# Two-stage attention with gated experts: four scored experts per token in more batches, and a new order of the program

## The chip, the core and the metric

The kernel runs on one core of one Trainium2 chip. The metric is device time in microseconds (us), as a median of runs. The engines of the core are named as in the profile: PE (matrix products, with PEld for its weight loads), DVE, ACT and POOL (elementwise work), and SP, whose queue issues all the DMAs.

## What is computed

```python
# x (8, 8, 512, 64), state (8, 8, 32, 64): attention both ways per batch and head
a = softmax(scale * x @ state.T);   xread = a @ state        # 512 rows
a2 = softmax(scale * state @ x.T);  sread = a2 @ x           # 32 rows
x = concat([xread, sread], axis=2) -> (8, 544, 512)          # B, S, D
# then per batch: four experts, of which each token takes the best two of its gate
logits = x @ w_gate; topk = 2 best; w = softmax over the 2 chosen
for e in range(4):
    q, k, v = x @ wq[e], x @ wk[e], x @ wv[e]                # 64 wide
    ye = softmax(causal(scale * q @ k.T)) @ v @ wo[e]
    out += (e chosen by the token) * w_of_that_choice * ye
```

The weights wq and wk are 200 times larger than drawn, so products are made from two float16 halves (high and low) in three matmuls: high*high, high*low, low*high.

## The kernel before

There are eight batches. A batch has 512 tokens in four query tiles of 128, numbered i = 0 to 3, and 32 rows of the state read, which are gathered over two batches into a tail. A batch goes through a **front** (state attention, products with the combined weights, the gate, the keys `kt`, the queries `qm`, the values `v`), a **main** part (scores, softmax, transposition, reads, output product) and a **side** (the state's own reads). The parts of neighbouring batches are interleaved.

In the main part, `probs` (L916) makes the score products of a *unit* into two PSUM banks. A *lane* of a unit is one query tile i against its 128*(i+1) keys. On each lane DVE adds the causal mask and takes the maximum (`masked`, L397, which writes `p`), ACT takes the exponential (`p<-p,mx`), and `split` (L338) writes high and low halves into `ph`: the high half on ACT, POOL or DVE, the low half on POOL or DVE. One DMA transposes `ph` into `pt`. `reads` (L957) multiplies `pt` with `v`, DVE or ACT scales the sums into `z`, and `result` (L1015) multiplies with `wo_n` and stores `o`.

There are two ways to score a tile, and `units_of` (L493) says which batch takes which:

```python
def units_of(b):
    if b < CFG["D1"]:
        units = [((0, "s"), (1, "s")), ((2, "s"),), ((3, "s"),)]
    elif b < CFG["DA"]:
        units = [((1, "d"),), ((0, "s"), (2, "s")), ((3, "s"),)]
    else:
        units = [((1, "d"),), ((0, "0"), (2, "0")), ((0, "1"), (2, "1")), ((3, "0"),), ((3, "1"),)]
    return units
```

- **Slots** ("s"): a token's two chosen experts sit in two slots, so a tile has two lanes. The query of a slot is a row of three candidates of which two are zeroed by the gate: DVE or ACT multiplies the product with the mask `m` (`qf`), `split` makes halves (`qh`), and a DMA transposes them into `qm`. A tile has 6 score matmuls of 128 rows and 6 of 64 rows, each 128*(i+1) columns wide (two of 64 rows run side by side on PE). A read per key tile is 6 matmuls of 194 columns.
- **All four** ("d", "0", "1"): a tile has four lanes, one for each expert ("0" and "1" are two of them each), and the weights of the two that were not chosen are zero only at the end. A tile's 12 score matmuls are all of 64 rows, the queries of a whole batch come straight from the product in transposed form, without `m`, `qf` and DMA, and a read per key tile is 12 matmuls of 65 columns.

`D1=6, DA=6` in `CFG` gives slots to batches 0 to 5 and all four to batches 6 and 7. A run of `st.run` (L255) issues the steps in a fixed order: the three strings in `ORDER` (L22) hold the order of the steps, which of several engines does a step that can go to more than one, and which buffer each tile takes. `FILL` (L511) lists matmuls on zeros that may be put where PE has nothing to do at the start.

Of the kernel before, what the change touches and what calls it, by code (L numbers as in the profile page):

```python
# [18 lines left out]
CFG = dict(FILL=(1.0, 1.4, 1.8, 2.2, 2.6, 3.0, 3.4, 3.8, 4.2, 4.6, 5.0,), RA=-1, RG=1, RV=2, RK=2, ZL=3, GP=1, PT=4, ZM=4, SM=4, QM=4, SIDE=32, FB=1, PX=1, PA=2, LB=1, xn=4, W0=-33, PACE=37.0, MU=2, XP=(1,), QP=(0,), LAG=2,
           FRONT=1.5, FSPAN=1.0, TSPAN=1.3, TOFF=1.2, KT=3, p32=3, ph=2, at=1, et=1, gs=1, xh=4, a2=1, o=4, sn=1, qf=2,  # L20
           n_eb=1, n_e2=1, n_a2t=1, n_xt_tail=2, n_z32=3, n_z=2, n_zh=2, n_tq=1, n_tv=2, n_tpt=1, n_tz=1, n_pt=3, D1=6, DA=6)
ORDER = (  # L22
    (
        "c-jrsgJKYB7y!`E|CZKJE!P@qORFurZM9|Fwr$(CZQHhO+xETZB~AhGf-H~^d>}CdKyHW+QIHkFAR%OiypRYALk0+ef{+!90RRF4gMdORh=A"
        "0P4c9;#NC2xK1`K>*E%-wcaF7E0AT1<^valLb!U`w@)u9CB#AQ$eGQkPRjiC^M<scbEVo4|uh4B<5g_>{@Vxa;Q!J?Q8D?%-(1o`na1VUvv1"
        "KFVpTmWx44+o$&cz`FwgQ}1ROTk%a0CnIT)P-u07cW9XD2Dam5~PDhPzYK>F31A~ur$<%Ah-+#aXG}n73cta;VNu_?AR6Z;WcOronR{z!f<Q"
        "`9ibZpLw86IyFh3^^ne`L4q8BGXah<sVFC7p=CBTWL1Wkr8=)`shJLUQx<C|ef<CYio4_{c4~wukUWWm&0T$zSxB*RJ1nhulya`KjGYo`sI0"
        ")9m5^N8zXfU*d@;C|dLn{~pBVi}RU^X}kbD#nifuXPrnTA0L91as;3QPo|Junvz!g8DpqhJNzf~hbXR^l|62dmJFO5$|zq%klb?!s-ThzlSd"
        "y`-^_17^TNh)<Pp7R-ckkbq`GeH;&oX%WQYF}M$L=uN9}F)V>K_y&Ba6gI$z;7d#45j=*qcn=;xWvqdB;0e5ir|=d0s0u!Vcklw<LrqLb&*3"
        "<HgjM_!>R>}`jHU4de1}?C6<<Lk{03#P2_~X-SR2b?HEfEX;0IL4pU@gV!$<0X>+w6iqh{C^JK+ZGh(D+ecE#rSo_;}RY=K7Yur9uaZs@2b_"  # L30
        "QLkq7kgtr^q~IO2kYSg9Eja<5N^c5cnG@S5Zr`AaTrd(;rIn6ViKB(sc5qFz~3+hKhRX1gst!o%)+EJ8z-Z~WYiO<VM-c<f5D&T;B-t)9+-k"
        "gU>cf>GcY;*15ZqfpC}#zj>NPy598x!8jFbO=nIWQ!UUL&I?;ISOpNm}J$0c`_?1FwGztb#SK5p}DGOzwWSE_@QW%BPVR%gexCOW2H_Ac&sJ"
        "I>9&{o`mdoUpelHpEFgu5|022nTKg-753?!{nwOF1b8W~LRq52MHn4`K#9guf_+QsPPMPJieyW~BYtgN|S(B0h@0sSfp|V;G3YLHL)BBXAL7"
        "Ud@TI82zJQ6h48)sVwKAx^x;#Pz06Z@_Y)XNH3~KA*ft|qbVcCQhiE=MX4g6LE}uAk9yNqPK~$l9D3sp&PCh!EEb^k97&E#QVfOSPR>i`@g;"
        "8H{8W${P;T1Jn|KX3q&T{Sx3Lth<#KcfUtxbL4zKYpUdGb&2G{Wwyo#II7k6<bPJ`F5GMA?^RE5h@1$v8NcpWR!1*}AVIDqb9Wok_~(1SN}W"
        "*kV(XbV@NLR6LdQckEwwWtZb!|L=NYfvL<OO2^8dGbYUPE9E>_oFscliE=Ws>-z~BgEsC`~iL0n|*K)wIn|tOw~9o4j~_o&qHY#CE!*xoOW}"
        "2>O&(a2`A(k(t-ByNJ`3wI1zuubhwvi%0fBF`}hDK=C9b1YVdx(kJb4I*JOVlO%E`Iyy9;-ib~pS8bf0#8Q;WlG)o@hc=F<-oKimFJep6hIh"
        "D+zB)CXE;|h9&spUH!;|VlR=2CuMEGucY{J;e?krvSs+DMBjjU?y!a-0`Z0bWH*X%fBVpSYTe!W$0YW%Q0WQwq+&n`kXn)ihj?Q*wIzg~7aq"
        "e&ZZjAX_O9|G^MW%WEhLzvmMi%2|0ig>g1sN11u5War6rl2dVBUQgkik27)(F2?Ej6sMKB@(gowCJy9C2!|;Y!P6v&BY7L;;#jVtx%oL3;?z"
# [1177 lines left out]
```

## Time and profile before

| | |
|---|---|
| median of 3 runs | 281.54 us (281.47 to 282.27) |
| profiled execution, its own time | 282.26 us |
| its span from first to last instruction | 280.5 us |
| time around the span | 1.76 us |
| granted TensorE clock | 1.00 in all of the span |
| PE, DVE, ACT, POOL busy | 96%, 90%, 82%, 60% of the span |

Busy time is the time in which at least one instruction of the engine runs. Durations of single instructions overlap with the next one's on DVE and ACT, so a sum of durations is larger than the busy time. The end of a matmul is modelled, so a start-to-start distance between groups of matmuls says more than a duration.

### The profile page before, as it was taken

What the parts mean: (1) busy time and instruction counts of PE and PEld (TensorE: products, weight loads), DVE (VectorE), ACT (ScalarE), POOL (GpSimd) and SP (SyncE); (2) the same over time, 40 slices, a digit from 0 to 9 for tenths busy, and PEclk for the clock granted to TensorE, in tenths of its full rate; (3) what the DMA queues carried; (4) which work ended last, traced back from release to release, by engine and by line L of the source; (5) the groups of instructions that cost most, each with busy time, mean ns of one, the idle gap of its engine ahead of it and who ended that gap; (6) DMA issues with size and microseconds to landing.
All of it is one profiled execution on the core that took longest, in us unless ns stands there. A gap on an engine that the chain in (4) does not pass through costs nothing.

```text
span 280.5 us, 9087 instructions
## 1 busy us (share of the span) xinstructions
PE 268.0 (96%) x3408; PEld 179.8 (64%) x3408; DVE 251.3 (90%) x749; ACT 229.0 (82%) x629; POOL 169.6 (60%) x234
## 2 busy tenths in 40 slices
PE   6979899899999899999999999999999999999995
PEld 3856666666486564767677566677576855576763
DVE  3599999999999999999999999899889999889852
ACT  3799898999899789899968988987886779877533
POOL 6534667177886787758757976595473587414210
PEclk9999999999999999999999999999999999999999
DMA  6957899999998969999999999995797979999995
GB/s 184 252 110 178 183 173 206 213 199 166 153 245 170 200 153 222 208 225 227 217 148 192 224 212 193 149 209 139 151 152 159 219 138 173 211 185 191 181 260 208
DMA packets 161804, 53.16 MB, mean 190 GB/s; under 512 B 140640, under 2 KB 157280, under 8 KB 161760
## 3 DMA queue, kind: packets, MB, share of 16 engines
q1 hardware_dynamic: 161760, 52.59, 96.7%
q8 instruction: 26, 0.43, 0.7%
q14 instruction: 18, 0.15, 0.2%
HBM read 11.02 MB, written 8.91 MB: 71 GB/s over the span
## 4 chain that ended last, share of the span: by engine, by line
PE 69%; DVE 17%; ACT 6%; DMA 4%; issue 2%; SPq 1%; DVEq 0%
PE bank L265 69%; DMA pt<-ph 2%; DVE gs L265 2%; DVE p L265 2%; DMA xn<-in_x_dram 2%; ACT e L265 1%; DVE xh L265 1%; DVE m L265 1%; DVE sbm L265 1%; DVE z L265 1%; DVE qf L265 1%; ACT qh L265 1%; SPq L265 1%; DVE xt_tail L265 1%; DVE eb L265 1%
## 5 line engine op out<-in xcount | busy, mean ns | idle before, releaser
L265 ACT ACTIVATE p<-p,mx 128x128 f32<-128x128 f32 (+3 forms) x80 | 41.7, 556 | 6.1 <-DVE su L265 2.4
L265 PE MATMUL bank<-gs,at 128*128 128x260 f16 (+3 forms) x320 | 44.0, 284 | 1.3 <-issue 0.8
L265 PE MATMUL bank<-v,pt 128*128 128x194 f16 (+1 forms) x600 | 42.2, 226 | 0.3 <-DMA pt<-ph 0.3
L265 PE MATMUL bank<-kt,qm 64*128 64x128 f16 (+7 forms) x384 | 42.2, 299 | 0.1
L265 PEld LDWEIGHTS <-pt 128*128 128x128 f16 x600 | 38.5, 98 | 4.0 <-issue 0.9
L265 POOL TENSOR_TENSOR ph<-p,ph 128x768 f16<-128x768 f32 (+1 forms) x18 | 34.7, 1925 | 4.7 <-ACT ph L265 2.3
L265 DVE CUSTOM_DVE_ANT_0 p<-bank,band 128x384 f32<-128x384 f32 (+3 forms) x80 | 36.2, 482 | 1.3 <-PE bank L265 1.0
L265 PEld LDWEIGHTS <-at 128*128 128x128 f16 x288 | 27.3, 97 | 7.9 <-issue 2.1
L265 PEld LDWEIGHTS <-qm 64*128 64x128 f16 (+1 forms) x384 | 21.0, 96 | 17.3 <-issue 8.7
L265 PE MATMUL bank<-at,gs 128*128 128x512 f16 (+1 forms) x116 | 30.0, 396 | 0.1
L265 PE MATMUL bank<-wo_n,z 128*128 128x512 f16 (+1 forms) x114 | 26.1, 368 | 0.0
L265 PE MATMUL bank<-wo_n,zp 128*128 128x512 f16 x84 | 20.4, 379 | 0.4 <-DVE xt_tail L265 0.4
L265 POOL TENSOR_TENSOR qh<-qf,qh 128x768 f16<-128x768 f32 x11 | 18.0, 1644 | 4.3 <-ACT qh L265 2.4
L265 ACT ACTIVATE o<-bank 128x512 f32<-128x512 f32 (+1 forms) x27 | 15.4, 578 | 6.4 <-DMA out_dram<-o 3.3
L265 DVE SCALAR_TENSOR_TENSOR xh<-xn,xh 128x512 f16<-128x512 f32 x26 | 18.6, 718 | 0.5 <-ACT xh L265 0.4
L265 ACT ACTIVATE ph<-p 128x1024 f16<-128x1024 f32 (+1 forms) x17 | 16.5, 970 | 1.9 <-DMA pt<-ph 1.8
L265 PEld LDWEIGHTS <-gs 128*128 128x128 f16 x108 | 9.9, 98 | 12.4 <-issue 2.4
L265 PEld LDWEIGHTS <-z 128*128 128x128 f16 x114 | 10.7, 98 | 10.9 <-issue 0.6
L265 ACT ACTIVATE z<-bank,c 128x64 f32<-128x64 f32 x72 | 16.0, 320 | 0.9 <-POOL c L265 0.8
L265 PEld LDWEIGHTS <-xh 128*128 128x128 f16 x416 | 14.0, 98 | 3.4 <-POOL xh L265 1.5
L265 ACT ACTIVATE xh<-xn 128x512 f16<-128x512 f32 x25 | 15.0, 621 | 1.1 <-DMA xn<-in_x_dram 0.7
L265 ACT ACTIVATE gs<-bank 128x260 f16<-128x260 f32 (+2 forms) x32 | 15.2, 500 | 0.5 <-PE bank L265 0.4
(241 smaller groups left out, 655.5 us busy)
## 6 DMA issues: line engine op xcount, KB each, us to landing
out_dram<-o SPq DMA_DIRECT2D x33, 256.0 KB, 3.0
xn<-in_x_dram SPq DMA_DIRECT2D x14, 512.0 KB, 4.6
xn<-in_x_dram SPq DMA_DIRECT2D x4, 256.0 KB, 3.8
sn<-in_state_dram SPq DMA_DIRECT2D x8, 64.0 KB, 3.9
p<-in_moe_wo_dram SPq DMA_DIRECT2D x2, 256.0 KB, 4.6
pt<-ph SPq DMA_TRANSPOSE x28, 4.8
p<-in_moe_wv_dram SPq DMA_DIRECT2D x1, 384.0 KB, 6.0
p<-in_moe_wk_dram SPq DMA_DIRECT2D x1, 384.0 KB, 4.7
```

The lines of the kernel that those rows point to most:

```text
L265: f(**{k: v.ap() if isinstance(v, View) else v for k, v in kw.items()})
```

## The change

`D1` goes from 6 to 3 and `DA` from 6 to 4: batches 0 to 2 keep slots, batch 3 scores tile 1 for all four experts and tiles 0, 2 and 3 by slots, and batches 4 to 7 score all four everywhere. `FILL` gets five more entries (5.4 to 7.0). `ORDER` is another set of strings: all steps may stand elsewhere, on another engine or in another buffer.

```diff
-CFG = dict(FILL=(1.0, 1.4, 1.8, 2.2, 2.6, 3.0, 3.4, 3.8, 4.2, 4.6, 5.0,), RA=-1, ...
+CFG = dict(FILL=(1.0, 1.4, 1.8, 2.2, 2.6, 3.0, 3.4, 3.8, 4.2, 4.6, 5.0, 5.4, 5.8, 6.2, 6.6, 7.0,), RA=-1, ...
-           n_eb=1, ..., n_pt=3, D1=6, DA=6)
+           n_eb=1, ..., n_pt=3, D1=3, DA=4)
 ORDER = (
     (
-        "c-jrsgJKYB7y!`E|CZKJE!P@qORFurZM9|Fwr$(CZQHhO+xETZB~AhGf-H~^d>}CdKyHW+QIHkFAR%OiypRYALk0+ef{+!90RRF4gMdORh=A"
+        "c-jrqgF+Z;7y!`E|JvG`+t%FBTwAM|wQ6pwS=DUYwr$(CZQHiZd(S(Z?2r?ZLTT`avJeKz004o2K|moLL_iAghQyE@0x<)uhLW%b)<SwHfLW"
...
```

What the two orders hold differently, counted over all rows: PE has 132 fewer reads of 194 columns (360 to 228) and 264 more of 65 columns (240 to 504), 48 fewer query products of 256 columns and 24 more of 512, and 5 more filling matmuls of 512 columns (11 to 16). The score matmuls are 384 before and after, but 54 of those with 128 rows become matmuls with 64 rows. The SP queue has 32 transpositions of `ph` for 28 and 6 of `qh` for 10; in blocks of 128 by 128 all transpositions are 1034 for 996.

DVE, the masks of batch 4's first unit before: tiles 0 and 1 by slots (four lanes of 128 and 256 keys, bank pairs by slot; numbers after a name are the buffer's).

```order
L265 ISA p_2_114,mx_163<-bank_83,band 128x128
L265 ISA mx_163 128x1
L265 RECIPROCAL su_172<-su_172 128x2
L265 ISA p_2_114,mx_163<-bank_83,band 128x256
L265 ISA mx_163 128x1
L265 ISA p_2_114,mx_163<-bank_77,band 128x256
L265 ISA mx_163 128x1
L265 ISA p_2_114,mx_163<-bank_77,band 128x128
```

DVE, the masks of batch 4's first unit in the changed program: tile 1 alone with all four experts.

```order
L266 ISA p_1_113,mx_163<-bank_81,band 128x256
L266 ISA mx_163 128x1
L266 ISA p_1_113,mx_163<-bank_81,band 128x256
L266 ISA mx_163 128x1
L266 ISA p_1_113,mx_163<-bank_83,band 128x256
L266 ISA mx_163 128x1
L266 ISA p_1_113,mx_163<-bank_83,band 128x256
L266 ISA mx_163 128x1
L266 TENSOR_TENSOR cmp_126<-lg_122 128x80
```

Four lanes of mixed width have become four of 256 keys, and the batch now has five such units and not three.

ACT, the exponentials of the same unit before, with the high half of `ph` as the last row.

```order
L265 ACTIVATE sbm_119<-sbm_119 128x32
L265 ACTIVATE p_2_114<-p_2_114,mx_163 128x256
L265 ACTIVATE z_1_167<-bank_80,c_0_173 128x64 x6
L265 ACTIVATE kt_137<-bank_81 128x512
L265 ACTIVATE lg_122<-bank_78 128x4
L265 ACTIVATE mx_162<-mx_162 128x2
L265 ACTIVATE lg_122<-bank_82 128x4
L265 ACTIVATE o_178<-bank_77 128x512
L265 ACTIVATE p_1_113<-p_1_113,mx_162 128x384
L265 ACTIVATE p_2_114<-p_2_114,mx_163 128x256
L265 ACTIVATE lg_122<-bank_80 128x4
L265 ACTIVATE ph_156<-p_2_114 128x768
```

ACT, the same unit in the changed program.

```order
L266 ACTIVATE p_1_113<-p_1_113,mx_163 128x256 x2
L266 ACTIVATE xh_94<-xn_89 128x512
L266 ACTIVATE p_1_113<-p_1_113,mx_163 128x256
L266 ACTIVATE xt_tail_154<-bank_84 64x4x32
L266 ACTIVATE o_177<-bank_83 128x512
L266 ACTIVATE p_1_113<-p_1_113,mx_163 128x256
L266 ACTIVATE gt_0_129<-gt_0_129 128x20
L266 ACTIVATE p_2_114<-p_2_114,mx_162 128x384
L266 ACTIVATE xh_94<-xn_89 128x512
L266 ACTIVATE xt_tail_154<-bank_84 64x4x32
L266 ACTIVATE p_2_114<-p_2_114,mx_162 128x384
L266 ACTIVATE ph_156<-p_1_113 128x1024
```

The unit's high half is now 1024 wide and not 768, and the next unit's first exponentials stand ahead of it.

PE at the start of the program before, around the transposition of the state `sn` (`band` is the filling matmul).

```order
L265 MATMUL bank_84<-ident,xn_89 128x128 x4
L265 LDWEIGHTS band
L265 MATMUL bank_83<-band 128x512
L265 MATMUL bank_81<-ident,sn_0_86 128x128 x2
L265 MATMUL bank_80<-ident,xn_90 128x128 x4
```

PE at the same place in the changed program.

```order
L266 MATMUL bank_81<-ident,xn_90 128x128 x4
L266 LDWEIGHTS band
L266 MATMUL bank_82<-band 128x512
L266 LDWEIGHTS band
L266 MATMUL bank_82<-band 128x512
L266 LDWEIGHTS band
L266 MATMUL bank_82<-band 128x512
L266 LDWEIGHTS band
L266 MATMUL bank_82<-band 128x512
L266 LDWEIGHTS band
L266 MATMUL bank_82<-band 128x512
L266 MATMUL bank_84<-ident,sn_0_86 128x128 x2
```

Five filling matmuls stand ahead of the state's transposition where one stood. Further on, ahead of the transposition of `eb`, four stand where three stood.

## Rows read from the trace of the kernel before

**Rows 1.** The page: span, and busy time by engine (share of the span, instructions).
```profile
span 280.5 us, 9087 instructions
PE 268.0 (96%) x3408; PEld 179.8 (64%) x3408; DVE 251.3 (90%) x749; ACT 229.0 (82%) x629; POOL 169.6 (60%) x234
```

**Rows 2.** The chain in order of time: start us, length us, engine and tile.
```profile
154.81 55.43 PE bank L265 x581
...
215.87 24.45 PE bank L265 x341
```

**Rows 3.** Stretches: length; busy PE, PEld, DVE, ACT, POOL; clock, DMA share, GB/s.
```profile
40.00:104.00 64.00, 60.64 (x810) 41.20 (x811) 62.50 (x174) 58.91 (x169) 44.22 (x50) 1.00 1.05 188
104.00:253.00 149.00, 148.18 (x1859) 98.54 (x1858) 139.70 (x441) 124.15 (x347) 98.31 (x118) 1.00 0.99 188
253.00:280.00 27.00, 24.35 (x278) 16.00 (x276) 18.23 (x61) 13.65 (x37) 5.38 (x10) 1.00 0.96 215
...
50.00:90.00 40.00, 38.30 (x472) 26.10 (x471) 38.90 (x111) 37.91 (x115) 26.79 (x32) 1.00 1.09 191
40.00:140.00 100.00, 96.59 (x1222) 64.51 (x1222) 97.85 (x279) 91.23 (x256) 71.46 (x81) 1.00 1.07 199
```

**Rows 4.** PE in order of time: start us, length us, op, out<-in, columns, count.
```profile
200.29 2.21 PE L265 MATMUL bank<-kt,qm 128*128 128x512 f16 x12
202.34 0.28 PE L265 MATMUL bank<-tl,rep 64*128 64x4 f32 x2
...
207.28 2.17 PE L265 MATMUL bank<-v,pt 128*128 128x194 f16 x24
209.39 0.83 PE L265 MATMUL bank<-kt,qm 64*128 64x256 f16 x12
...
237.88 1.63 PE L265 MATMUL bank<-v,pt 128*128 128x65 f16 x48
239.45 1.47 PE L265 MATMUL bank<-kt,qm 64*128 64x512 f16 x12
240.85 1.47 PE L265 MATMUL bank<-wo_n,z 128*128 128x512 f16 x6
```

**Rows 5.** Groups by form: out<-in, shapes, count | busy us, mean ns | idle before.
```profile
L265 ACT ACTIVATE ph<-p 128x1024 f16<-128x1024 f32 x10 | 10.6, 1062 | 1.8 <-DMA pt<-ph 1.8
L265 ACT ACTIVATE p<-p,mx 128x512 f32<-128x512 f32 x20 | 14.0, 721 | 0.2
L265 ACT ACTIVATE p<-p,mx 128x128 f32<-128x128 f32 x20 | 7.6, 395 | 2.0 <-DVE mx L265 1.1 <-POOL mx L265 0.8
L265 ACT ACTIVATE o<-bank 128x512 f32<-128x512 f32 x25 | 14.6, 594 | 6.0 <-DMA out_dram<-o 3.3 <-PE bank L265 2.7
L265 ACT ACTIVATE qf<-bank,m 128x64 f32<-128x64 f32 x36 | 8.0, 320 | 1.0 <-PE bank L265 0.7 <-DVE m L265 0.3
L265 DVE CUSTOM_DVE_ANT_0 p<-bank,band 128x512 f32<-128x512 f32 x20 | 13.2, 681 | 0.2 <-PE bank L265 0.2
L265 DVE CUSTOM_DVE_ANT_0 p<-bank,band 128x128 f32<-128x128 f32 x20 | 5.6, 283 | 0.4 <-PE bank L265 0.4
L265 DVE TENSOR_SCALAR o<-bank 128x512 f32<-128x512 f32 x8 | 5.5, 683 | 0.3 <-PE bank L265 0.3
L265 POOL TENSOR_TENSOR ph<-p,ph 128x1024 f16<-128x1024 f32 x9 | 19.2, 2132 | 0.9 <-ACT ph L265 0.8
L265 POOL TENSOR_TENSOR qh<-qf,qh 128x768 f16<-128x768 f32 x11 | 18.0, 1644 | 4.3 <-ACT qh L265 2.4 <-DVE qh L265 1.7
L265 PEld LDWEIGHTS <-pt 128*128 128x128 f16 x600 | 38.5, 98 | 4.0 <-issue 0.9 <-DMA pt<-ph 0.4
```

**Rows 6.** PE at the start, in order of time, with its idle time before.
```profile
5.44 0.38 PE L265 MATMUL bank<-band 128*128 128x512 bf16 x1 [0.23 <-ACT xT L265]
6.56 0.44 PE L265 MATMUL bank<-ident,sn 128*128 128x128 f32 x2 [0.74 <-ACT sn L265]
...
17.03 0.66 PE L265 MATMUL bank<-ident,eb 128*128 128x128 f32 x4 [1.16 <-DVE eb L265]
```

**Rows 7.** The only matmul that waited for a transposition, and these transpositions' landing (us).
```profile
248.23 0.91 PE L265 MATMUL bank<-v,pt 128*128 128x65 f16 x24 [0.32 <-DMA pt<-ph]
...
pt<-ph SPq DMA_TRANSPOSE x28, 4.8
```

More of the change, by code (lines that the diff above doesn't have):

```diff
@@ L17 @@
 AX = mybir.AxisListType
[L19 removed]
+CFG = dict(FILL=(1.0, 1.4, 1.8, 2.2, 2.6, 3.0, 3.4, 3.8, 4.2, 4.6, 5.0, 5.4, 5.8, 6.2, 6.6, 7.0,), RA=-1, RG=1, RV=2, RK=2, ZL=3, GP=1, PT=4, ZM=4, SM=4, QM=4, SIDE=32, FB=1, PX=1, PA=2, LB=1, xn=4, W0=-33, PACE=37.0, MU=2, XP=(1,), QP=(0,), LAG=2,
@@ L25 @@
[L25 to L39, printed above, removed]
@@ new lines @@
+        "mgRDdLq5eyu}0}qG~sbC#sg4D1P(m-0s3<;nb_<;{pgdE@tQIG|yLkLDgD4vD-Py;GKF{}#3u_lzmLKp%KpcI~mhHwsQK^WGC3(yGaz(u$Mk"
+        "x&9l;#G(NPe=%fzzga^X-o;1;3zbO!gv`fLp>-4*PsZ-LNmAyaj+lCU~{+u9pEOchboW@8bfQi1)CupibGj!0%hPf9D-i36}G_^XbVNL4HU#"
+        "<upPR>4#*Ghs5cydPS6e7!9fVZ7SJAou_Nq(Q!ohngQHfk2{yn|><l|$07T$&90+$H99zO&=mLFUFf7B}a1X}95QtAhAqrREK3Ik2u`gtUaW"
+        "D)#XctU`l^Bf`a5bKW;m{A>(+D^W-C;V6go?NZk3az!1#59M%!H{h25R6msD$gV2i%8QP#Gt|45*1!a5jvGTDTY1<78M2Jz*g{f(cLx=0I{<"
+        "0#l$W#-q8g2<F2)NJPh>0WJV9S_)5~HpXINS_Vm|4mQNc5Q#6~0mR`mXoN|r2|k4lxRsy7LuiamF&S;dYPcL)U|n1RFJUFThI&{XTVgZ(2zg"
@@ new lines @@
+        "->dQ)?J1NHG06ouT-3VY!hcnc}$9ejqA)D=@vYmCA7unImw2TV<Uunm5JZrB}r<2U#P9dQtTg>sO924jEx07Gy94#e*;6o=stXp5c{3O#T*Z"
+        "pIP#2Rh*v{tY9sGtR?N_?brI7@UfKVJ3FLX*eIhP*40u3vd?xq@R$GrsF~c{7z|T5eCBy%mV??7yrQrT8v*QBaOwh)DJ(>Y|KPIs2z^Od@u)"
+        "ns68TPriu86eo;C~Pvg-OeQ611ARqiq3Gpvwq3)Cjz3>ywMZ&~50rOE0+JaeW8}_6?nuLN|F&p)w{4^Q=kv}ED>{Nh)$&aRBA?i&9Nil$u;t"
+        "4QJi$RnQ9j3<|6c3Z(c07tFfiWi?M-SYA8Soh9`akPA%!qq%C!WAf+=q7KD#=aRF%zD`z7!ubBl1b?M|tQp5<AXI%$-&E0w%y+XuKDTlkyq#"
+        "!+6|;qWJ*sM_=quHFzK9z=Ghx2QfM3#6wt<<MUap#knwocJg`5jU{M5$5LU~#kIL2?cu|ifOm6Kx`>6TGF73X6iS{vh)Pm3I>1#aj`ngMtVE"
@@ new lines @@
+        "6J2<FAoRF>Z1AudnFs2mNZB2<Q=D3a=MG_90slnP5xb*e${u_lGkL9Rs~ur7C?)c6rQQEjS2b*UcJrv`KhxAA3cPFb)84WNNkfev$P%7<65G"
+        "u_AST#vKjRoua!uqB028!8VSDFr6vecXx?u|FQ+F7yCXVng!cBJdeg@I&lM*YFEAq5!PVk1&Q(aX1a9#GH~-^L1=XNw^z%^9WieN4Xs(<r}y"
+        "~hR|aiNy+#o9_I#p3)jnS97Ut)7@y%Wbb?RwSZYsa`6S=LU-%V&<0<}wTcwMpk>tEV((q7vf<8Qq#!*_{E<VzbpW;S&hUs`SPoT82fX?xFN`"
+        "sB~8&0J3Jc(j>GOeX4w1^hdR9Z+&=sc&BZBl}l(lpv3D`+`g;AOOuw$UoekLhKTl;n&27ccQ@x{IaxAFii$v{Op)2Fk#fc@yoR)l!Cmkh1f1"
+        "+D>caJFb-s;>-7Nvt;C*<i{H+7iW}Rw1%$m56r@4IX7>n8I+&%aRJUG{v5~wT#$n}nDcNUevU+$xI7o;yquMHQ&BF*#dsza=Mc`p**KIda|P"
@@ new lines @@
+        "Z)IXR4HQAKWMRk$kelFU4tA~~F|GSe-N;A(u0_tS0uiF>3v&!Ih3iC^PxIY61^E+3@5bcgp!Hry}QIf`H40lC2k<qaO99xCK3_jn)elbd`<v"
+        "Wn7iDg=k=ung3f7|SOJwV#rnr2EX;gd1}^j^hX1lzVGOJtC*5ziy>wEP9%b&{65B$)%}1;$zZ+AG2zE?#<2lxOC!Hd_r1sM;@RLxixp-N0dV"
+        "Pa4$VWow*x#;WpftUvM_@mb3JVvq)P$N~TZvG4<pAJV=vBAAQC_@Py9M04~C>`6(TvRPu}xi8nfZ$w{TJKBtuOhLg!a9>nJ*o_fhUPAy;fq$"
+        "HN}^nowPC3!)o<gyIm?);Wt(na~mKlu|6)@#(2pK}jBEkpS|5981Ll!tRU`Oar#1oz}u^ou<-Tn2M_IV)lEo4@jPijc1QhpS6l1Np`kq?>lv"
+        "it?A+*$pzfOi@xvqNRqs#m@GFt4K|WuUDuS57C=cSx{=pEjlN!iDanOl~LNkMsg$Z)Z0`~{_!v!#Z_e)57#@yGFq=vtc=i3+E^k*q_&LF_SR"
@@ new lines @@
+        ";ew!tddM$2uxt+M5@LN3HMSxG%<<?OWGwlK?Ur!3Si*<CwhRjjZ(XFs*7-LZTYZddHAMc8F4Z};q~wbd6EY3J>}&9q;7%`TX~&9&=R%^K?in"
+        "`f`Bf>pQKR?1zpSN6tkSY0dae(NkN;mWw1)<oyqLVIktY=KR+#Wu$tSxNWO(3N#>EyO*vP`AV?+9Hcla({H1)w3s7&i&O7w!*^PbPIP&EyCq"
+        "@E3Ld^7poOqQ?2MKxu-V6;<U0;SH%U`JBzYsR@Hs9_g2k)wMZwffUE8TU6hM<tL(XbvijD*8k)J!=G-#-V#}?a)^PD$P4~@ex$jonHL@6s?^"
+        "av1)pcvEj$3Q%%)`}l>#dg6cR%c>#aaUQ%YNHG&2OGAwM*j~xb|AZ3Rs-^xU}w%rE`f~dY8c^bQxVk=j9T+Brd7T<Qlmc7wh6&GMC)dwhmg;"
+        "8XH(0`)f@sg=_4xxF+tOHFYUnW|!50%jU8>Kj-Vva=2zLr}K8XTq>8(HFvpP3+L|wTppL#{RbG@s!;"
+    ),
@@ new lines @@
+    (
+        "c-pO%?G}R|3`4nj|A*d0CT(fa?aUt&CnQb!VQb-{{pGq~bUt$Zk`gH+p4&O@ym#qb3^c|eh|J7=E8m3hZ;3&yxFNnCp;-5jx^W2_enhAZm%2"
+        "x|keWeJIBU#_JXlUr-U{<B+x1_L7@NljU`m!jUDq2j!AiYJPLD~C3*4I;Y>eVm*f`^5twpd28M$Jc0tOYWtiM*(@#1;HCTf^kus((zqEr-Hk"
+        "3vN-+tgtv#jS9~THx^nBr9gOz(32CNM1j9zc^j~rqz_mUz^*eFCJjUwz*R>-YzUzc|q3gJSAz*^a~K@zz`mW+lWdbe&2c1<xKuhA3%&a@@9D"
+        "faGwD>"
+    ),
+    (
+        "c-mEyixz`02t#@I|NnS5RChK#&K4;l3G4p7W-QI@@RSyRSGbiOceg0zl;?!8we;2*4?9C*P7>$9w?w%sHL@(&b%c9TM_F!TlNAb#>$rK5(B@"
+        "!RPbr6|)8ZUgAM6B1fg<kg`T|XKQ0HvzEPVlqR6&gcY?(?k5D2k$$`Wj$_!em(TyQYlAkEW{*K<PTd6iO&KAtN_sU9MC>e42Sy@{f&C=S(af"
+        "xKM$KDHv>3P(8G+6t3=b!ncD10ug7Ync?;77ISmZnej;7%^BSMaHt{>mm|&9m8q&S6GkRK;A<n^?u-nNR6y1@sOkPf6Jff6{tn*kyBkH>vfh"
+        "Hx(i4CS6$5&{QIn}&P3&%xg$$KRu_#y7TY3cbEj+;ESI9>0AB8I##Ru|uvbikYd&<LcU>1N`n6coVRsHzCY4zlYpuH0v@6PQoz-44@rpa6m_"
+        "q<6B)v3kXJPUC(ARL-o>1FP%FJppJ1MK55uqw7Nc<>GvhU2OC+^~ZAVslSvZr19cRm0b;q9vO1D8_<cK"
```

40 lines of the change are left out of this document (11 added, 29 removed).

## The prediction, made before the changed kernel ran

> **What bounds the kernel now.** I read the page first [rows 1]: the span is 280.5 us, PE is busy for 96% of it, DVE for 90% and ACT for 82%. The chain that ended last, in order of time, says where PE is the bound [rows 2]: one piece of 55.43 us from 154.81 and one of 24.45 us from 215.87 are nothing but PE. Then the table of stretches [rows 3]. Between 104 and 253 us PE is busy 148.18 of 149 us, DVE 139.70, ACT 124.15 and POOL 98.31; the granted clock is 1.00. Between 40 and 104 us it is DVE that is full, 62.50 of 64 us (97.7%), and PE waits for 3.4 us. After 253 us the elementwise engines run dry (DVE 18.23 of 27 us) and PE ends the kernel. Batches 4 and 5 and the tile of batch 3 lie between 104 and 253 us, so what the change is worth is read from that stretch: PE has 0.8 us of idle time there, DVE 9.3 us, ACT 24.9 us.
>
> **PE's share of the change.** Reads: 24 reads of 194 columns take 207.28 to 209.39 = 2.11 us, 87.9 ns each; 48 reads of 65 columns take 237.88 to 239.45 = 1.57 us, 32.7 ns each [rows 4]. 132 fewer of the first save 11.6 us, 264 more of the second cost 8.6 us: -3.0 us. Scores: tile 3 by slots takes 200.29 to 202.34 = 2.05 us, tile 3 with all four experts 239.45 to 240.85 = 1.40 us [rows 4]. That is 0.65 us for four blocks of 128 keys, 0.1625 us a block. Two whole batches have 10 blocks each and tile 1 of batch 3 has 2: 22 blocks, -3.6 us. The query products go from 48 of 256 columns to 24 of 512, the same 12,288 columns, at no cost. Together PE loses 6.6 us of work, all of it in a stretch where it is 99.5% busy.
>
> Each read of 65 columns has a weight load of 128 columns of its own, whose mean duration is 98 ns [rows 5]; 264 more of these pairs is what could speak against the change. But 48 pairs go at 32.7 ns each [rows 4], so the loads are hidden and do not set the pace, and -3.0 us stands. The Trainium skill, TensorE: Matmul & The Clock Gate, section Back-to-back issue gap, speaks against this: it gives about 81 ns per matmul of 128 columns in a sustained stream of load and matmul pairs. An estimate by that page, with 81 ns as a floor for a pair, is 264 x 81 ns = 21.4 us for the new reads, so that PE would gain 9.8 us of work from them and not lose 3.0. The 48 pairs in the trace, at 32.7 ns, do not agree with such a floor, and the trace decides.
>
> The five filling matmuls: one is 0.38 us long, some 0.2 us when another follows it. Four of them stand where PE idled 0.23 and 0.74 us around the state's transposition, one where it idled 1.16 us [rows 6]. I take zero. If the cover were gone it is 1.1 us, and nothing is gained either, since the clock is 1.00 already.
>
> **The elementwise share.** The score lanes grow from 80 to 98 (24, 26, 24, 24 of the four widths instead of 20 each). For the masks that is 4 x 0.283 us up to 4 x 0.681 us [rows 5], with the two widths between 8.5 us on DVE, and 1.5 us for 18 more reads of the maximum. The exponentials cost 4 x 0.395 up to 4 x 0.721 us [rows 5], together 9.9 us on ACT. The halves of `ph` become 26 pieces of 1024 and 6 of 768, from 16 and 12; ACT takes 10 more high halves of 1024 at 1.062 us (+10.6), POOL 6 more low halves at 2.132 us (+12.8). Against it go 7 of POOL's `qh` halves at 1.644 us (-11.5), 18 of ACT's `qf` pieces at 0.320 us (-5.8), and DVE hands six output copies of 0.683 us (-4.1) to ACT, which pays 0.594 us each (+3.6) [rows 5]. Summed in this way over all forms whose count differs, 65 on DVE, 39 on ACT and 35 on POOL: DVE +1.4 us, ACT +14.4 us, POOL about +2 us. On ACT neighbouring durations overlap: its durations add up to 280.8 us against 229.0 us busy for 629 instructions, 82 ns each, so 13 more instructions take 1.1 us off. ACT's busy time grows by 13.3 us, nearly all of it in the same stretch, since batches 0 to 2 and 6 to 7 keep their work.
>
> **DMAs.** SP issues four more transpositions of `ph` and four fewer of `qh`; in blocks there are 38 more, 4%. One of 16 blocks lands after 4.8 us, and in the whole trace one read waited for one, 0.32 us [rows 7]. The cost is between zero and 38/16 x 4.8 = 11.4 us, if each were waited for in full. I take zero, which is nearest to the waits seen; what is hidden behind reads that come one or more units later stays hidden unless the queue itself falls behind.
>
> **The sum.** Three bounds on the new length of the 149 us:
> - PE: 149 - 6.6 = 142.4 us, if it stays as busy as it is.
> - DVE: 139.70 + 1.4 = 141.1 us of work. At its best rate, 97.7% (40 to 104 us), that takes 144.5 us: 4.5 us less than now.
> - ACT: 124.15 + 13.3 = 137.45 us of work. The best rate that ACT shows over a long stretch is 37.91 of 40 us, 94.8% (50 to 90 us) [rows 3]. At that rate it takes 145.0 us: 4.0 us less than now.
>
> The longest decides. PE stops being the bound and ACT, with DVE close behind, takes its place; of PE's 6.6 us some 4.0 us reach the end. The head (to 104 us) and the tail (from 253 us) hold the same kinds of work as before, and I take them as unchanged; a new order can move each by about 1 us either way, which goes into the range. The span becomes 280.5 - 4.0 = 276.5 us, and with 1.76 us around it the profiled execution would take 278.3 us. The profiled execution before, 282.26 us, lies 0.72 us above the median of 281.54 us, so on the median's scale the forecast is 281.54 - 4.0 = **277.5 us**.
>
> **Rivals.**
> - PE stays the bound. The work of DVE and ACT can be pulled across the edges of the stretch (after 253 us DVE is idle 8.8 us and ACT 13.4 us [rows 3]), and POOL, at 66%, can take more. Against it: DVE would have to run at 141.1/142.4 = 99.1%. All 6.6 us arrive: 274.9 us.
> - Three engines cannot all be near full. The best sum of PE, DVE and ACT in any of these stretches is 182.05 of 64 us, 2.845 engines (40 to 104 us); the stretch now has 412.03/149 = 2.765 [rows 3]. Afterwards there are 148.18 - 6.6 + 141.1 + 137.45 = 420.1 us of work; at 2.845 they take 147.7 us. Only 1.3 us are left: 280.2 us.
> - Slower: ACT saturates at its ordinary rate. Exponentials, the high halves and the copies out of PSUM all queue on ACT in order, and every bank that it empties late holds up PE. Over 40 to 140 us it ran at 91.23 of 100 us [rows 3]. At that rate 137.45 us take 150.7 us, 1.7 us longer than now: 283.2 us. It decides from 137.45/149 = 92.2% downwards.
> - Weight loads are no longer hidden behind the short reads. If each pair took the 98 ns of its load [rows 5], 264 pairs would take 25.9 us against the 11.6 us saved, and PE's sum would be +14.3 - 3.6 = +10.7 us: 292.2 us. The 48 reads of the trace say no [rows 4]. (The rule of the Trainium skill weighed above is this mechanism.)
>
> That the change does not do what it says is excluded by the counts in the order.
>
> **How the numbers follow.** Forecast (276.2 to 279.2 us) 0.42; PE stays the bound, 0.22; three engines, 0.19; ACT slower, 0.15; weight loads, 0.02. A measurement of this kernel can tell about 0.3%, 0.84 us, from no change. Faster by more than that (below 280.7 us) are the first two cases and about half of the third: 0.74. Within it: the rest of the third, 0.09. Slower: 0.17. For eight in ten the range runs from 273.6 us, PE's full gain with 1.3 us from a better head, to 282.4 us, which leaves out the two slow cases.
>
> **What the changed profile would show.** Reads of 65 columns in groups of 48 at 1.5 to 1.6 us, and PE's busy time 5 to 6 us lower (6.6 us less work, 1.1 us more filling), show PE's term. DVE near 253 us and ACT near 242 us busy show the elementwise terms; ACT at about 95% between batch 3 and the last scores, with PE's idle time there growing from 0.8 us to some 3 us behind ACT or DVE, shows the bound. PE without such gaps means the first rival, gaps above 5 us the second or third. More than a few tenths of waiting for `pt` would make the DMA term wrong. A later start of the first scores, or a longer tail after the last of them, would make wrong what I took as unchanged.

## The result and the profile after

The changed kernel takes 285.62 us (median of 5 runs, 283.62 to 286.97) against 281.54 us: a ratio of 1.0143, 95% interval 1.0099 to 1.0187. It is slower, and lies 3.2 us above the end of the predicted range. Its profiled execution took 285.03 us, 1.8 us of it around the span.

The page of the changed kernel: span, busy time by engine, and in 40 slices PE's clock in tenths.

```profile
span 283.2 us, 9349 instructions
PE 266.6 (94%) x3521; PEld 173.3 (61%) x3521; DVE 250.5 (88%) x757; ACT 241.2 (85%) x642; POOL 177.2 (63%) x240
...
PEclk9999999999999999999999999998999999999999
```

Against [rows 1] PE is busy 1.4 us less, DVE 0.8 us less, ACT 12 us more and POOL 7.6 us more, and the span is 2.7 us longer. One slice of 40 has a lower clock. The stretches of [rows 3], after (columns as there):

```profile
40.00:104.00 64.00, 58.46 (x785) 39.69 (x784) 60.98 (x163) 57.48 (x159) 46.79 (x62) 1.00 1.05 187
104.00:253.00 149.00, 145.55 (x1941) 92.03 (x1942) 140.61 (x451) 134.40 (x366) 104.39 (x119) 0.99 1.04 193
253.00:280.00 27.00, 26.10 (x326) 16.17 (x320) 18.99 (x72) 18.41 (x48) 2.14 (x5) 1.00 1.02 212
...
190.00:200.00 10.00, 10.00 (x137) 5.84 (x137) 7.92 (x24) 5.94 (x18) 6.37 (x7) 0.83 1.04 190
```

In 104 to 253 us ACT is busy 90.2%, DVE 94.4% and PE 97.7%: no engine is full. Two groups of PE, the scores of the last tile of batch 2 and the last scores of the program, cut the span into three. They start at 110.74 and 251.73 us before, at 111.21 and 252.74 us after. So the head is 0.5 us longer, the part between is 141.5 us instead of 141.0, and the tail behind the last scores is 30.5 us instead of 28.8. The forecast for the middle was 141.0 - 4.0 = 137.0 us: 4.5 us of the miss lie there, 0.5 in the head and 1.7 in the tail, together the 6.7 us between the forecast of 278.3 us for the profiled execution and its 285.03 us.

### Where the middle lost its time

PE in order of time (start us, length us, ..., in brackets the idle time before and who ended it), then DVE and POOL at the same place.

```profile
186.71 1.24 PE L266 MATMUL bank<-wo_n,z 128*128 128x512 f16 x5
189.94 0.94 PE L266 MATMUL bank<-xT,bd 64*32 64x512 f16 x24 [1.99 <-DVE bd L266]
190.81 4.31 PE L266 MATMUL bank<-wo_n,zp 128*128 128x512 f16 x12
```

```profile
186.28 0.40 DVE L266 CAST at<-et 128x512 f16<-128x512 f32 x1
186.78 2.58 DVE L266 TENSOR_TENSOR at<-et,at 128x512 f16<-128x512 f32 x1
189.28 0.41 DVE L266 TENSOR_TENSOR z<-bank,c 128x256 f32<-128x256 f32 x1
189.62 0.27 DVE L266 SCALAR_TENSOR_TENSOR bd<-bank,bd 128x128 f16<-128x128 f32 x1
```

```profile
186.51 0.23 POOL L266 TENSOR_TENSOR c<-su,wgt 128x4 f32<-128x4 f32 x1 [0.49 <-DVE su L266]
186.69 2.12 POOL L266 TENSOR_TENSOR ph<-p,ph 128x1024 f16<-128x1024 f32 x1
```

DVE's low half of `at` takes 2.58 us. The other one of the same form in this trace takes 0.68 us (the group of two has a mean of 1630 ns). POOL's low half of `ph` began 0.09 us earlier and ends at 188.81, and only 0.55 us after that does DVE's end: DVE stood still for about 1.9 us. The Trainium skill, SBUF — State Buffer, section Who interferes with whom, has a rule for this: a DVE instruction with two inputs in SBUF contends with a POOL instruction that reads SBUF, for ports that only one of them can hold at a time. The trace agrees: 1.9 us of waiting beside 2.12 us of POOL. The recorded starts alone do not tell which of the two has to wait: at 142.21 us POOL's `wd` also starts 0.09 us ahead of DVE, which runs two `xh` there in 1.28 us, their ordinary time, and it is `wd` that takes 1.82 us, where POOL's `c` of the same 128x4 takes 0.20.

Behind it the loss grows. DVE reaches `bd` late, PE idles 1.99 us, and after that gap the granted clock is 0.83 in 190 to 200 us, that is partly at the lower of the two levels. The twelve products behind the gap take 4.31 us. ACT then waits 3.29 us for PE's banks before its next output copy at 193.59.

### The profile page after: what moved, and what is told of

Read it like the earlier page. It is cut to its first block, busy times and chain, and to the rows that moved or that the text cites. A ratio compares the mean times of both kernels' runs of the same rounds, so it can differ in the third digit from the quotient of the medians.

```text
span 283.2 us, 9349 instructions
## 1 busy us (share of the span) xinstructions
PE 266.6 (94%) x3521; PEld 173.3 (61%) x3521; DVE 250.5 (88%) x757; ACT 241.2 (85%) x642; POOL 177.2 (63%) x240
## 4 chain that ended last, share of the span: by engine, by line
PE 55%; DVE 26%; ACT 8%; DMA 4%; issue 3%; POOL 1%; SPq 1%; DVEq 0%; POOLq 0%; ACTq 0%
PE bank L266 55%; DVE p L266 4%; DVE xh L266 2%; DVE eb L266 2%; DMA tpt<-ptl 2%; DMA xn<-in_x_dram 1%; DMA pt<-ph 1%; ACT gs L266 1%; DVE mb L266 1%; DVE kt L266 1%; DVE sbm L266 1%; ACT a L266 1%; DVE m L266 1%; DVE qf L266 1%; DVE at L266 1%
## 5 line engine op out<-in xcount | busy, mean ns | idle before, releaser
L266 ACT ACTIVATE p<-p,mx 128x384 f32<-128x384 f32 (+3 forms) x98 | 50.9, 555 | 2.1 <-POOL mx L266 1.2
L266 POOL TENSOR_TENSOR ph<-p,ph 128x1024 f16<-128x1024 f32 (+1 forms) x21 | 42.4, 2017 | 15.4 <-ACT ph L266 8.3
L266 DVE CUSTOM_DVE_ANT_0 p<-bank,band 128x256 f32<-128x256 f32 (+3 forms) x98 | 43.5, 480 | 0.9 <-PE bank L266 0.6
L266 PE MATMUL bank<-kt,qm 64*128 64x384 f16 (+7 forms) x384 | 38.6, 299 | 1.7 <-ACT kt L266 1.5
L266 PE MATMUL bank<-v,pt 128*128 128x65 f16 (+1 forms) x732 | 39.2, 211 | 0.0
L266 PE MATMUL bank<-gs,at 128*128 128x260 f16 (+3 forms) x272 | 38.3, 287 | 0.9 <-DVE mx L266 0.6
L266 ACT ACTIVATE ph<-p 128x1024 f16<-128x1024 f32 (+1 forms) x24 | 24.6, 1024 | 0.4 <-DMA pt<-ph 0.2
L266 ACT ACTIVATE gs<-bank 128x512 f16<-128x512 f32 (+2 forms) x33 | 15.9, 506 | 0.6 <-PE bank L266 0.5
L266 ACT ACTIVATE v<-bank 128x256 f16<-128x256 f32 x35 | 13.0, 391 | 2.4 <-PE bank L266 2.2
L266 POOL TENSOR_TENSOR eb<-eb,sbm 128x512 f32<-128x512 f32 (+1 forms) x8 | 12.4, 1551 | 2.9 <-DVE sbm L266 1.9
```

The lines of the kernel that those rows point to most:

```text
L266: f(**{k: v.ap() if isinstance(v, View) else v for k, v in kw.items()})
```

## The experiments

**Without the collision.** The low half of `at` moves from DVE to POOL, where it stands ahead of that low half of `ph`, so that the two run one after the other.

```diff
-DVE  TENSOR_TENSOR at<-et,at 128x512   (the low half of batch 6)
+POOL TENSOR_TENSOR at<-et,at 128x512
```

> The changed program with one step on another engine: the low half of at of batch 6 (the DVE instruction that took 2.58 us from 186.78, where another one of the same shape takes 0.68 us and POOL's low half of ph ran from 186.69 to 188.81) goes from DVE to POOL, where it stands ahead of that low half of ph. Theory (one stretched instruction): PE's idle 1.99 us at 188 goes, PE's clock stays at 1.00 and the products at 190 to 195 lose no time (1.6 us); the span falls by 3 to 4 us from 283.2 to about 279.6 us, the median from 285.6 to about 282. Rival (DVE and ACT are full anyway, so PE's gap is only where their lateness shows): the gap moves to another place and the span falls by less than 1.5 us, to 282 us or more.

Measured: 283.16 us, ratio 1.0064 (1.0037 to 1.0090). The gap is gone, the twelve products take 2.76 us, and the profiled execution (span 280.1 us) has a mean clock of 1.00. The stretches of e1_port:

```profile
150.00:215.00 65.00, 64.68 (x893) 41.24 (x890) 62.70 (x208) 62.38 (x169) 51.17 (x56) 1.00 1.09 192
...
104.00:253.00 149.00, 147.09 (x2000) 93.70 (x2000) 141.73 (x470) 137.74 (x373) 106.10 (x122) 1.00 1.10 197
```

The middle falls from 141.5 to 137.9 us. So in the two traces 3.6 us of it were the collision and what it brought with it: shown. The edit also takes 0.68 us of work off DVE; l_dve below, with 9.6 us off DVE, says that this is worth little. On the ratios of the medians the gain is smaller, 0.8% or 2.2 us, where 3.6 us had been expected. What remains is 0.6% slower than before. In the trace the head is 0.9 us longer than before and the tail 1.7 us, which eats 2.6 of the 3.1 us that the middle gained; the other runs of e1_port show clocks from 0.994 to 0.999 and spans up to 2.2 us longer. The runs that follow ask whether more was to be had.

**Fills.** The five added filling matmuls are taken out, alone (e2_fills) and with e1_port's edit (f_new).

```diff
-CFG = dict(FILL=(..., 5.0, 5.4, 5.8, 6.2, 6.6, 7.0,), ...
+CFG = dict(FILL=(..., 5.0,), ...
```

> The changed program without five of its filling matmuls: four of the five that stand ahead of the state's transposition at 5.8 us and one of the four at 15.7 to 17.0 us, so that eleven are left as before the change. Theory (they cover idle time): the state's transposition stays at 7.1 us or comes 0.1 to 0.3 us earlier, the span changes by less than 0.5 us. Rival (they delay the head): the span falls by 1 to 1.5 us. Rival (they hold the clock): the granted clock falls below 1.00 in the head and the span grows by 1 us or more.

> e1_port and e2_fills together: the low half of at on POOL, and eleven filling matmuls in place of sixteen. Theory (the five cost the head about 1 us when the clock holds): the median falls by 1 to 1.5 us against e1_port (283.2), to 281.7 to 282.2 us, with single runs 5 us or more above it in which the granted clock falls in the head. Rival (they only cover idle time): within 0.5 us of e1_port.

Measured: e2_fills 284.32 us, 1.0095 (1.0061 to 1.0129), in an interval that overlaps that of the changed kernel; f_new 284.36 us, 1.0073 (1.0031 to 1.0116), as good as e1_port. So no cost of the fills is seen. Whether they hold the clock in the head stays open: it was 0.82 from 10 to 40 us in the profiled execution of e2_fills, at 290.25 us the longest of its runs, and 1.00 there in that of f_new.

**Work in front of PE's gap.** PE's groups of `wo_n,zp`, six products each, which stood behind the late `xT,bd`, are put ahead of it: both of them (e4_pe_swap), or only the first (e5_one_group).

```diff
+MATMUL bank<-wo_n,zp 128x512 x6
 MATMUL bank<-xT,bd 64x512 x24
-MATMUL bank<-wo_n,zp 128x512 x6
```

> The changed program with two groups of six output products (wo_n,zp, 512 columns) moved ahead of the product xT,bd on PE, so that PE has 2.6 us of work while DVE makes bd late; the DVE and POOL orders are untouched and DVE's stretched instruction of 2.58 us stays. Theory (what costs time is PE's idle 1.99 us and the clock that falls behind it): the gap at 188 us goes, the clock stays at 1.00, the span falls by 2.5 to 3.6 us, to about 280 us. Rival (DVE's 1.9 us are what is lost, since DVE is 98% busy there): the span falls by 1 us or less, and PE waits for DVE later on.

> The changed program with one group of six output products (wo_n,zp, 1.3 us) moved ahead of the product xT,bd on PE; the DVE and POOL orders are as they were, and DVE's instruction of 2.58 us stays. Theory (the clock falls behind the idle 2 us and costs another 1.6 us): PE's idle time there is cut to some 0.7 us, the clock stays at 1.00, and the span falls by 1.5 to 2 us although DVE is as late as before. Rival (PE waits for DVE's lateness anyway): the idle time moves to the next wait, the span changes by less than 0.7 us.

Measured: e4_pe_swap 288.37 us, 1.026. It says nothing, since its result is not that of the program any more: probably the second group writes a bank before an output copy has read it, and ACT's waits are other ones. e5_one_group 285.53 us, 1.0109 (1.0072 to 1.0146). Its PE at that place:

```profile
186.87 1.46 PE L264 MATMUL bank<-wo_n,z 128*128 128x512 f16 x6
190.92 1.46 PE L264 MATMUL bank<-wo_n,zp 128*128 128x512 f16 x6 [2.59 <-DVE gs L264]
192.31 0.84 PE L264 MATMUL bank<-xT,bd 64*32 64x512 f16 x24
```

The group in front waits itself, for DVE's late `gs`. Behind this gap of 2.59 us the clock is 1.00 (185 to 200 us) and six products take 1.46 us, yet the time is that of the changed kernel, with a clock of 0.79 at another place, 64 to 72 us. The lateness of DVE costs the time, not the place of `xT,bd`.

**Other orders.** The whole order behind 14 us was searched anew by a model with in-order queues, for the changed scoring and the old one (o_after, o_before); only the steps between 40 and 112 us (w_new on e1_port, w_old on the kernel before); and all steps, by a search that asks for slack (r_new, r_old). Only the order strings differ.

> The changed program with the same steps, engines and buffers, but with the steps of each engine put in another order (from 14 us on), searched with a model of the engines' queues that takes its durations from the traces, among them that a DVE and a POOL instruction of the colliding kinds exclude each other; the mean over slightly disturbed durations was to be short. Theory (the new scoring is worth its 4 us and the order given with it loses them): with an order as carefully searched as that of the next kernel, this one is shorter than it by 3 to 6 us, and PE's idle time falls from 16.6 us to 12 us or less. Rival (DVE and ACT take the gain, whatever the order): the two kernels are within 1.5 us of each other. Rival (orders searched so don't hold on the chip): both are as long as the orders they start from, or longer.

> The kernel before with the same steps, engines and buffers, in an order searched in the same way, with the same number of trials, as the kernel above. Theory (the new scoring is worth 4 us): shorter than the kernel before, and longer by 3 to 6 us than the changed program in its searched order. Rival (the elementwise engines take the gain): within 1.5 us of it.

> The changed program with the step of e1_port on POOL, and with only those steps put in another order that start between 40 and 112 us (some 490 steps, batches 0 to 3; same engines, same buffers). The new order was searched with a model of the engines' queues that now also has waits of an engine for its own results and the length of the DMA queue as the traces show them. Theory (the order given with the new scoring loses 2 to 3 us in batches 0 to 2, whose scoring has not changed: PE's waits of 0.85, 0.66, 1.48, 0.64, 0.79 and 0.89 us between 57 and 105 us): the waits there shrink, and the span falls by 2 us or more against e1_port, from 280.1 to 278 us or less. Rival (DVE, 95% busy there, sets the pace and PE's waits cost nothing): the span stays within 1 us of e1_port. Rival (what is gained there is lost behind it, between 112 and 253 us): PE's waits there grow by as much.

> The kernel before with only those steps put in another order that start between 40 and 112 us, searched in the same way. It is the control for the kernel above. Theory (the order of the kernel before was already good in this stretch): it gains 1 us or less against the kernel before. Rival (such a search gains in any order): it gains as much as the kernel above does against e1_port.

> As w_new, but with all steps from 14 us on free, and searched for orders that stay short when durations differ by 4% and DMAs by 25%. Theory (the new scoring is worth 4 us, the order hides it): 277 us or less, and 3 us or more below r_old. Rival (the elementwise engines take the gain): within 1.5 us of r_old. Rival (such orders don't hold on the chip): 285 us or more.

> The kernel before with all steps from 14 us on free, searched as r_new, with the same number of trials. Theory: 3 us or more above r_new. Rival (the elementwise engines take the gain of the new scoring): within 1.5 us of r_new. Rival (such orders don't hold on the chip): 285 us or more.

Measured: o_after 310.0 us (1.0956), o_before 314.9 (1.1112), w_new 283.92 (1.0103, 1.0041 to 1.0166), w_old 288.97 (1.0269), r_new 292.82 (1.0397), r_old 291.56 (1.0365; part of its output is wrong for a cause not found, so its time is an indication only). Orders made by such a model do not hold on the chip, for either scoring, so they cannot say which scoring is better: o_after is 4.9 us shorter than o_before, r_new 1.3 us longer than r_old. One thing can be read: w_new, in whose trace PE's listed waits between 40 and 112 us add up to 5.0 us instead of the 6.1 of e1_port, gains nothing at the end.

**The old head.** The steps of the first 20, 40 or 60 us go in the order of the kernel before, the rest as in e1_port with the old fills.

> f_new with the first 20 us in the order of the kernel before: the steps that start within its first 20 us stand in its order, on its engines, ahead of all others; the others follow in the order of the changed program. Theory (the start of the changed program is late by about 1 us: DVE and ACT have done 0.8 and 1.0 us less work after 10 us, 1.0 and 1.5 us less after 40 us): the span falls by about 1 us against f_new. Rival (lateness in the start is made up later): within 0.4 us of f_new.

> As h_20, with the first 40 us in the order of the kernel before. Theory (what the new order loses ahead of the changed batches is lost in their cause, the order of the first batches): the span falls by 1.5 to 3 us against f_new, to 280 us or less on the median's scale, so that the new scoring begins to show. Rival (the loss lies between 40 and 104 us, where the order stays that of the changed program): no more than h_20 gives.

> f_new with the steps that start within the first 60 us of the kernel before put at its times, between the others at the times of the changed program, and on its engines. Theory (the loss lies between 40 and 104 us too): 2 to 4 us below f_new, 279.5 us or less. Rival (two orders don't fit together at the seam): above h_40, and PE waits by 1 us or more more than in f_new between 50 and 80 us.

Measured: 285.6 us (1.0153), 284.3 (1.0098, 1.0060 to 1.0135) and 287.62 (1.0163), against 1.0073 of f_new. The old head brings nothing back: either the lateness is made up later, or the seam costs as much; the runs do not separate the two.

**Which engine sets the length.** From e1_port some 9 us of work are taken off one engine between 104 and 249 us, or off all three.

```diff
+LEFT = (490, 493, 505, ...)     # steps: l_act 17 output copies on ACT, l_dve 16 low halves on DVE
+THIN = (489, 492, 504, ...)     # groups: l_pe, 22 groups of six products on PE
 for n in memoryview(steps).cast("H"):
+    if n in LEFT:
+        continue
     s = self.all[n]
-    for f, kw in s["ways"][ways[n]][2]:
+    calls = s["ways"][ways[n]][2]
+    for f, kw in calls[:2] + calls[4:] if n in THIN else calls:
```

> e1_port with less work on ACT: 17 of the output copies that ACT makes between 104 and 249 us are left out (those rows of the output are not made, their stores move old data). ACT loses 17 x 0.594 us less the overlap of 0.08 us each = 8.7 us. Theory 'ACT at its ordinary rate sets the length' (the slower rival): the time falls by 5 us or more, to 278 us or below. Theory 'PE still sets it, ACT and DVE only cost single waits': within 1.5 us of e1_port (283.2). Theory 'all three are coupled, and none alone is the bound': 1 to 3 us shorter, 280 to 282.

> e1_port with less work on DVE: 16 low halves of kt and xh (128x512) between 104 and 209 us are left out, so that old low halves are used. DVE loses 16 x 0.68 us less the overlap of 0.08 us each = 9.6 us. If DVE sets the length: 5 us or more shorter. If PE does: within 1.5 us of e1_port (283.2). If ACT does: the same, within 1.5 us. If all three are coupled: 1 to 3 us shorter.

> e1_port with less work on PE: in 22 groups of six products of 512 columns (18 output products and 4 of the front, 104 to 249 us) the two middle products are left out, so these sums lack a part. PE loses 22 x 2 x 0.213 = 9.4 us. If PE still sets the length: 7 us or more shorter, 274 to 276. If ACT or DVE sets it: less than 2 us shorter. If all three are coupled: 1 to 4 us shorter, with PE waits growing by the rest.

> e1_port with all three cuts at once (17 output copies of ACT, 16 low halves of DVE and 44 products of PE left out): 8.7, 9.6 and 9.4 us less work on the three engines. If these three engines' work sets the length of the stretch, whichever ends last: 7 to 9 us shorter than e1_port, 274 to 276. If the order of waits (transposition DMAs, POOL, banks) sets it: clearly less, 4 us or below.

| run | ratio to the kernel before | 95% interval | in us, against e1_port |
|---|---|---|---|
| e1_port | 1.0064 | 1.0037 to 1.0090 | |
| l_act | 1.0043 | 1.0003 to 1.0083 | -0.6 |
| l_dve | 1.0006 | 0.9968 to 1.0045 | -1.6 |
| l_pe | 1.0035 | 0.9988 to 1.0083 | -0.8 |
| l_all | 1.0054 | 1.0009 to 1.0099 | -0.3 |

The last column is the difference of the ratios times 281.5 us; e1_port was not run beside the other four, but each ratio is to runs of the kernel before made beside it. The intervals overlap, so at most a microsecond or two was gained; no span of the four traces (280.5 to 281.9 us) is below the 280.1 us of e1_port. The work is really gone, as the stretch from 104 to 253 us shows, in l_act, l_dve, l_pe and l_all in this order:

```profile
104.00:253.00 149.00, 146.69 (x1980) 92.88 (x1980) 141.00 (x466) 129.86 (x355) 105.77 (x121) 1.00 1.09 195
```

```profile
104.00:253.00 149.00, 146.93 (x2011) 93.58 (x1996) 133.36 (x453) 137.04 (x373) 102.57 (x123) 1.00 1.09 197
```

```profile
104.00:253.00 149.00, 139.76 (x1941) 89.64 (x1941) 140.74 (x467) 136.53 (x372) 105.17 (x121) 1.00 1.10 194
```

```profile
104.00:253.00 149.00, 139.63 (x1944) 89.16 (x1937) 133.14 (x450) 129.53 (x355) 102.37 (x122) 1.00 1.10 195
```

PE drops to 139.8 us of 149 in l_pe, 7.3 us less than in e1_port, and each engine that was relieved simply idles more. In l_all all three have 9 to 20 us to spare, and the time stays. So in e1_port the work of neither PE nor DVE nor ACT alone sets the length, nor that of the three together. POOL, at 102 to 106 of 149 us, is not full either. What does not move in these rows is the column before the last: the DMA share, 1.09 to 1.10 in each, where the kernel before had 0.99 [rows 3].

The chain that ended last says how this fits together. In e1_port it is PE for 73% of 104 to 253 us and holds no DMA there; in l_all PE is 24% and DMAs are 31 of 149 us. Pieces of it (start us, length us, engine and tile), in e1_port and in l_all:

```profile
108.85 50.72 PE bank L264 x609
184.84 25.29 PE bank L264 x307
```

```profile
132.25 20.89 PE bank L269 x280
156.72 6.09 DMA pt<-ph
193.67 5.71 DMA a2t<-a
216.91 7.24 DMA pt<-ph
232.18 12.11 DMA pt<-ph x2
```

So behind PE's path lies a second one, about as long, that goes through the transpositions and comes forward as soon as the engines have less to do.

The issues of the SP queue in l_all, in order of time (start us, length us):

```profile
153.09 2.07 SPq L269 DMA_TRANSPOSE pt<-ph  x1
155.21 1.41 SPq L269 DMA_DIRECT2D out_dram<-o  x2
156.72 3.58 SPq L269 DMA_TRANSPOSE pt<-ph  x1
160.34 0.58 SPq L269 DMA_DIRECT2D out_dram<-o  x1
160.97 0.63 SPq L269 DMA_DIRECT2D sn<-in_state_dram  x1
161.71 1.26 SPq L269 DMA_TRANSPOSE xT<-xh  x1
163.08 1.22 SPq L269 DMA_TRANSPOSE z<-zh  x1
164.40 2.96 SPq L269 DMA_TRANSPOSE pt<-ph  x1
```

Here the queue goes from one issue into the next; there is hardly a tenth of a microsecond between them. By the starts and ends of all its issues in the traces, overlaps counted once, it issues for 61.3 of the 65 us from 150 to 215 in l_all, 59.4 in e1_port and 50.8 in the kernel before; over 104 to 253 us it is 138.5, 134.6 and 124.0 us, so that 10 us of idle time are left in l_all and 14 in e1_port. The number of issues hardly differs there (90, 93, 90). What grew are the transpositions of `ph`, 23 instead of 19, from 42.8 to 57.5 us in e1_port. The issues of `pt<-ph` in the kernel before, e1_port and l_all (ns: shortest/median/longest), and the landing in l_all:

```profile
L265 SPq DMA_TRANSPOSE pt<-ph x28: 1280/2025/3357, 47.9 to 264.8; - x28
```

```profile
L264 SPq DMA_TRANSPOSE pt<-ph x32: 1326/2312/3704, 48.8 to 265.9; - x32
```

```profile
L269 SPq DMA_TRANSPOSE pt<-ph x32: 1333/2428/3757, 48.2 to 267.0; - x32
...
DMA to landing us min/median/max: 4.3/4.9/7.2
```

One issue holds the queue for 1.3 to 3.8 us. If each is paired with the low half of `ph` that ended before it, the median is 1.5 us for pieces 768 wide, in all three kernels, and for pieces 1024 wide 2.7 us before, 2.4 in e1_port and 2.5 in l_all. So an issue of one size has not become longer; the median of all grows because 26 of 32 pieces are wide ones now and 16 of 28 were. What makes one wide piece take 1.6 us and another 3.8 stays open. The DMA queue's own row on the page (packets, MB, share of 16 engines) before, and in l_all:

```profile
q1 hardware_dynamic: 161760, 52.59, 96.7%
```

```profile
q1 hardware_dynamic: 166624, 53.83, 102.5%
```

And with three engines relieved, waits for these transpositions come up that the kernel before hardly had ([rows 7] has one of 0.32 us on PE's matmuls). In l_all, what the instructions on `pt` waited for, and who waited for the transposition (us, times):

```profile
  DMA pt<-ph: 4.4, 9
...
  ACT ph L269: 3.9, 5
  PEld L269: 2.8, 5
  PE bank L269: 1.6, 4
```

That less work on PE, DVE and ACT does not shorten e1_port by more than a microsecond or two is shown by these runs. That SP's queue with its transpositions holds it is argued from these rows. Two rivals are left: the 16 DMA engines behind the queue, whose share rose with it, and the order of waits through all engines, since even in l_all the queue has idle time and more than half of the chain between 104 and 253 us is neither PE nor DMA, but short pieces of DVE and ACT. A kernel with fewer transpositions and the same orders was not run, and it stays open how many microseconds that would give.

## Why the prediction was wrong

On the scale of the profiled execution 6.7 us were missed. The first step that failed is POOL's work, put at "about +2 us" and priced at nothing for the other engines: one of its instructions stopped DVE, which with what followed cost 3.6 us of the middle. The second is the head and tail, "unchanged": 2.2 us. The other 0.9 us lie in the rates of the middle. On top of that, l_all shows that the rule behind the forecast, that the longest of three engines' work decides, is not what sets the length.

**PE's work: right.** Reads went from 42.2 to 39.4 us of busy time (-2.8; forecast -3.0), the scores from 53.2 to 50.0 (-3.2; forecast -3.6). The reads, after (out<-in, shapes, count | busy us, mean ns | idle), and a group of them in order of time (start us, length us):

```profile
L266 PE MATMUL bank<-v,pt 128*128 128x194 f16 x228 | 21.3, 247 | 0.0
L266 PE MATMUL bank<-v,pt 128*128 128x65 f16 x504 | 18.1, 194 | 0.0
...
249.84 1.63 PE L266 MATMUL bank<-v,pt 128*128 128x65 f16 x48
```

Forty-eight reads of 65 columns take 1.63 us, as in [rows 4], so their weight loads stay hidden: the fourth rival is out, and so is the estimate made by the page TensorE: Matmul & The Clock Gate of the Trainium skill. The five fills cost 1.5 us of busy time (forecast 0, bound 1.1) and no length that the runs show. As a whole PE is busy only 1.4 us less, where 5 to 6 were forecast, and 3.7 us less in e1_port: between the two lie 2.3 us, of which 1.6 are products `wo_n,zp`, slower behind the gap.

**The elementwise sizes: right for ACT and DVE, wrong for POOL.** ACT is busy 241.2 us (forecast 242), DVE 250.5 (forecast 253; 248.1 without the collision). The new lanes were priced well by their rows [rows 5]. POOL went from 169.6 to 177.2 us, +7.6 and not +2.

**The rates: the step that failed most, by one event that no sum of work contains.** "The longest decides" gave 137.0 us for the middle; in the changed kernel it is 141.5, and 3.6 us of that go with the collision. I counted POOL's extra work as some 2 us of an engine with room, and did not ask with which DVE instructions the longer low halves of `ph` would collide. PE's idle time between 104 and 253 us grew from 0.8 to 3.4 us, which the prediction took as a sign of its bound; but 1.99 us of it are this one gap. That e1_port has 137.9 us in the middle, close to the forecast, is luck: by the same rule l_all, with 9 us less work on each of the three engines, would have to be some 9 us shorter than e1_port, and it is 0.3.

**DMA, "I take zero": too little looked at for what was left to gain.** I costed the 38 additional blocks by the waits seen, while PE was still the bound and hid them, and named the condition, "unless the queue itself falls behind", without looking at the queue's own load. It issued for 83% of the stretch before, for 88% in the changed kernel and for 90% in e1_port, and with work taken off PE, DVE and ACT the length stays. No PE instruction of the changed kernel waits for `pt<-ph`, as forecast, and no DMA is in its chain between 104 and 253 us, so for the changed kernel itself zero is not refuted; but such a check cannot see a second path that is about as long. That this path is the queue is argued, not shown.

**Head and tail "unchanged": wrong by 2.2 us.** The tail after the last scores has 26.4 us of PE work instead of 25.6 and 4.1 us of idle time instead of 3.15; it is 30.5 us in e1_port as well. Why the new order leaves more for it stays open. The old head put back did not help (h_20 to h_60), and the 0.5 us in the head are not explained either.

**The rivals.** "ACT at its ordinary rate", 283.2 us, came nearest, and ACT's rate in the stretch is indeed 90.2%, below the 92.2% from which it was to decide. But the mechanism is not the one at work: 8.7 us less work on ACT (l_act) gives 0.6 us. In part ACT's rate is low because it waited 3.29 us for banks of a PE that waited for DVE; without the collision it is 92.4%. "Three engines cannot all be near full" is refuted: in e1_port, from 150 to 215 us, (64.68 + 62.70 + 62.38)/65 = 2.919 engines are busy, more than the 2.845 that I took as the most. "PE stays the bound" falls with l_pe, although PE is 73% of the chain of e1_port. The chance of 0.17 for slower was too small because all rivals came from work per engine; a single collision and a fall of the clock behind it were none of them, nor a path through the transpositions.
